# Attention and SwiGLU block on one core: where copies and additions of the query projection are queued

## The chip, the core and the metric

The kernel runs on one core of a Trainium2 chip. A core has five engines that work side by side, each through its own instructions in order: TensorE (PE in the profile; PEld is its weight load), VectorE (DVE), ScalarE (ACT), GpSimd (POOL) and SyncE (SP), which here only issues DMA transfers; ScalarE issues some too. Engines wait for each other by semaphores. The metric is the device time of one execution in microseconds (us), as the median of several runs.

## What is computed

A transformer block of 2048 rows and width 1024, in bfloat16, with six modulation vectors made from a condition `c`:

```python
mod = (_silu(c) @ w_mod).reshape(c.shape[0], 6, 1, -1)
sa, ca, ga, sb, cb, gb = ...
h = _layernorm(x) * (1 + ca) + sa
x = x + ga * _A_ref(h, A_k_cache, A_v_cache, A_wq, A_wo)
h = _layernorm(x) * (1 + cb) + sb
x = x + gb * _B_ref(h, B_w_gate, B_w_up, B_w_down)
```

`_A_ref` is attention with 32 query heads of 128 and 4 key/value heads, over the last 512 positions of the cache; `q = x @ wq`, scores, softmax, times `v`, times `wo`. `_B_ref` is a SwiGLU network, `silu(x @ w_gate) * (x @ w_up) @ w_down`, with an inner width of 3584.

## The kernel before

The rows are worked in four chunks of 512. Each chunk takes the 32 heads in turn, so the attention loop has 128 iterations `i` (`ch, h = divmod(i, Hq)`, from L1135); after head 31 of a chunk comes the output projection (`oproj_plain` in chunk 0, `oproj` after that). The network follows in two stretches of 1024 rows. This text is about the loop.

**The query projection.** From the eighth head on, the projection is made for two heads at once by a scheme of seven products in place of eight (Strassen's, in a variant with fewer additions). `product(p0, m)` (L677) issues product m for the heads p0 and p0 + 1 as four 128x256 matmuls. It takes quarters of the weights, or sums of quarters: `weight_sums` (L646) makes four sums per group of four heads on VectorE, k = 0 to 3, each a 128x1024 subtraction (the line of the helper, L644). The input's sums are made once a chunk by `input_sums` (L669), at heads 27 and 28 for the next chunk.

In chunk 0 all four weight sums of a group are computed, and three of them are also stored to memory (`store_sums`, L658). Chunks 1 to 3 use the same weights again: they fetch the three kept sums (`load_sums`, L662, 768 KB) and compute only the sum k = 1, which needs the fetched k = 0 sum.

The products meet in two PSUM banks, QBK and XBK. Products 1, 6, 5 and 3 add up one after the other in QBK, and after each the running partial sum is copied out: after 1, 6 and 5 to float32 tiles `sn` (`snap`, L702), after 3 straight to the query tile `q` (in `q_fourth`, L740). Products 2, 7 and 4 go to XBK, and VectorE adds a kept partial sum to each (`q_add`, L708; the row is L710). The tracker keeps whole banks apart: a product that writes a bank waits until the copy or addition that reads it is done.

**An iteration's order.** It is written out by hand, and a pair of iterations works for the pair of heads p0, four heads ahead of the scores. Even: `q_first` (the product 4 and its addition that the pair before left in `late`; then product 1, copy), scores of head i + 1 (four 128x512 matmuls), first exp (L764, half of the scores), `q_second` (product 6, copy; product 2, addition), second exp, then `pv` (sixteen 128x129 matmuls for head i, then VectorE's reciprocal L780 and multiplication L781). Odd: `q_third` (product 5, copy; product 7, addition), scores, first exp, `q_fourth` (product 3, copy to `q`; product 4 is left for later), second exp, `pv`. Since every engine works in order, the place of a call in this text is its place in the engine's queue.

Beside these, `run()` and `step()` advance background tasks by one step after `q_first` or `q_third`: layer norms of the next chunk (L428, L376, L377, L437, L392) and the modulation vectors (L1010, L1014), all VectorE. A finished modulation vector goes through `mod_columns` after an odd iteration's `pv`, by matmuls into QBK and a copy out: L1031 on ScalarE for `ga` and `gb`, L1038 or L1041 on VectorE for the others.

**Which engine copies.** `LEAD` is 4 and `Hq` 32. The copies after products 1 and 5 are on ScalarE throughout. Those after products 6 and 3 are on ScalarE while p0 < 36, that is in chunk 0, and on VectorE after that (L706, L748).

**Where sums and loads are queued.** At the end of an iteration, behind `pv` and its multiplication: in chunk 0 one of a group's four weight sums per iteration (L1210 to L1213), and in chunks 1 to 3, every fourth iteration, `load_sums` (L1206 to L1208). In SP's queue that load stands behind `oturn(i - 1)`, a transposing DMA which waits for the multiplication of the head before.

Of the kernel before, what the change touches and what calls it, by code (L numbers as in the profile page):

```python
# [4 lines left out]
AF = mybir.ActivationFunctionType  # L5
# [113 lines left out]
def bass_adaLN_cond__sliding_block_cached__swiglu_ffn__prompt_kernel(  # L119
# [16 lines left out]
    Hq = A_wq.shape[1] // Dh  # L136
# [10 lines left out]
    HG = Hq // 4  # L147
# [9 lines left out]
    T = _Tracker()  # L157
    V, A, G, TE, SP = nc.vector, nc.scalar, nc.gpsimd, nc.tensor, nc.sync
    PE = _Stream(nc.alloc_semaphore("s_pe"), TE, self_exempt=True)
    ACT = _Stream(nc.alloc_semaphore("s_act"), A)  # L160
    DVE = _Stream(nc.alloc_semaphore("s_dve"), V)
# [68 lines left out]
    for i in range(4):  # L230
        for ap_l, b_l, nm, n in ((st_sb, B_st, "st", 12), (mv_sb, B_mv, "mv", 2), (rs_sb, B_rs, "rs", 2)):
            ap_, b_ = small("%s%d" % (nm, i), n, F32)
# [9 lines left out]
    def bank(b, n=512, off=0):  # L242
        return ps[:, b * 512 + off:b * 512 + off + n]
# [18 lines left out]
    with nc.Block() as block:  # L262

        @block.gpsimd
        def _(g):
# [380 lines left out]
            def weight_sums(g, st, e, which):  # L646
                sl = g % NWQ
                w_, bt = wq_sb[sl], B_tq[sl]
                t_ = [tq_[sl][:, n] for n in TQ_AT]
                b11, b12, b21, b22 = w_[:, 0:4, 0:256], w_[:, 0:4, 256:512], w_[:, 4:8, 0:256], w_[:, 4:8, 256:512]  # L650
                for k in which:
                    x, y, extra = ((b12, b11, []), (b22, t_[0], [bt[0]]), (b22, b12, []), (b21, t_[1], [bt[1]]))[k]
                    tt_(st, e, t_[k], bt[k], x, y, ALU.subtract, B_wq[sl] + extra)
# [8 lines left out]
            def load_sums(g):  # L662

                if g >= NCH * HG:
                    return
                ap, bb = kept_sums(g)
                T.op(Q_tq[g % NWQ], lambda: SP.dma_start(ap, wq_t[g % HG]), reads=[B_wqt[g % HG]], writes=bb)
# [31 lines left out]
                        rhs, hb = h_[:, hk, lo:lo + 256], B_h[slot][hk]  # L699
                    mm(out_, lhsT, rhs, kc == 0 and m in (1, 2), kc == 3, [lb, hb], PB[b], loose=True)  # L700

            def snap(st, k):  # L702
                if st is ACT:
                    T.op(ACT, lambda: A.activation(sn[k], bank(QBK, 256), AF.Copy), writes=PB[QBK] + [B_sn[k]])  # L704
                else:
                    T.op(DVE, lambda: V.tensor_copy(sn[k], bank(QBK, 256)), writes=PB[QBK] + [B_sn[k]])  # L706

            def q_add(i, half, off, k):  # L708
                dst = q_sb[i % NQ][:, half * 256:(half + 1) * 256]
# [6 lines left out]
            def q_first(p0):  # L716
                if late:
                    late.pop()()
                if p0 >= NA:
                    return  # L720
                product(p0, 1)
                snap(ACT, 0)

            def q_second(p0):
                if p0 >= NA:
                    return
                product(p0, 6)
                snap(ACT if p0 < Hq + LEAD else DVE, 1)
                product(p0, 2)
                q_add(p0, 0, 0, 0)  # L730

            def q_third(p0):
                if p0 >= NA:
                    return
                product(p0, 5)
                snap(ACT, 2)
                product(p0, 7)
                q_add(p0 + 1, 1, 256, 2)

            def q_fourth(p0):  # L740
                if p0 >= NA:
                    return
                product(p0, 3)
                dst, b_ = q_sb[(p0 + 1) % NQ][:, 0:256], B_q[(p0 + 1) % NQ]
                if p0 < Hq + LEAD:
                    T.op(ACT, lambda: A.activation(dst, bank(QBK, 256), AF.Copy), writes=PB[QBK] + [b_])
                else:
                    T.op(DVE, lambda: V.tensor_copy(dst, bank(QBK, 256)), writes=PB[QBK] + [b_])  # L748

                def last():  # L750
                    product(p0, 4)
                    q_add(p0, 1, 256, 1)

                late.append(last)
# [373 lines left out]
            mod_rest = mod_task([m for k_ in ("cb", "sb", "gb") for m in mods[k_]])  # L1128
            next(mod_ga)
            tasks.append(mod_ga)  # L1130
            ln1 = {}
            ln2 = {}
            o_list = [(k, p) for k in range(2) for p in range(8)]
            o_done = []
            for i in range(NA):  # L1135
                ch, h = divmod(i, Hq)
                p0 = i - i % 2 + LEAD
                if ch == 0 and h in (13, 17, 22):
                    load_wo((13, 17, 22).index(h))
                if ch and h % 2 and 5 <= h < 5 + 2 * AHEAD[ch]:  # L1140
                    load_unit(ch, h // 2 - 2)
                at_xl = [AT_XL + 2 * j for j in range(3)]
                if h == 0 and ch + 1 < NCH:
                    ln1[ch + 1] = ln_task(range((ch + 1) * TPC, (ch + 2) * TPC), False, at_xl, (AT_N, AT_N + 2),
                                          scale=(g1, B_g1, sa, B_sa))
                    tasks.append(ln1[ch + 1])
                if ch == NCH - 1 and h == 3:
                    ln2[0] = ln_task(range(TPC), True, at_xl, (AT_N, AT_N + 2), scale=(g2, B_g2, sb, B_sb))
                    tasks.append(ln2[0])
                if ch == NCH - 1 and h == 10:  # L1150
                    finish(mod_rest)
                    ln2[1] = ln_task(range(TPC, 2 * TPC), True, [AT_FT + 2 * j for j in range(4)],
                                     [AT_MS + 2 * j for j in range(4)], turn=False)
                    tasks.append(ln2[1])
                if ch == NCH - 1 and h == 29:
                    for g_ in list(tasks):
                        finish(g_)
                    for a_ in kept:
                        ln_turn(*a_)
                if h == 26 and ch + 1 < NCH:  # L1160
                    finish(ln1[ch + 1])

                if i + LEAD < PLAIN:
                    qproj(NOP + i // 2, (XBK, QBK)[i // 2], i % 2)
                    if i + LEAD == PLAIN - 1:
                        load_wq(3)
                elif i % 2 == 0:
                    q_first(p0)
                else:
                    q_third(p0)  # L1170
                if ch == 0:
                    for g_ in [ln1[1]] * (i > 3) + [mod_ga] * (i > 2) * (1 if i < 8 else i % 2 if i < 20 else 1 + i % 2):
                        step(g_)
                elif h not in (Hq - 5, Hq - 4):
                    run()
                if i + 1 < NA:
                    scores(i + 1)
                if p0 >= PLAIN:
                    if i % 2 == 0:
                        q_second(p0)  # L1180
                    else:
                        q_fourth(p0)
                exps(i + 1, 2)
                g = (i + 5) // 4
                if i % 4 == 3 and HG + 2 <= g < NCH * HG:
                    weight_sums(g, DVE, V, (1,))
                if h == Hq - 5 and ch + 1 < NCH:
                    input_sums((ch + 1) % 2, (0, 1))
                if h == Hq - 4 and ch + 1 < NCH:
                    input_sums((ch + 1) % 2, (2, 3))  # L1190
                if p0 >= NA:
                    for _ in range(4):
                        o_done.append(o_list[len(o_done)])
                        o_first(ch, *o_done[-1])
                pv(i, mod_columns if i % 2 else lambda: None)
                if i >= 1:
                    oturn(i - 1)
                if i < 3:
                    input_sums(0, ((0, 1), (2,), (3,))[i])
                if i == 1:  # L1200
                    weight_sums(2, DVE, V, (0, 1))

                g = (i + 1) // 4 + 2
                if i % 4 == 3 and i > 3:
                    load_wq(g)
                g = i // 4 + 2  # L1206
                if i % 4 == 0 and g >= HG + 2:
                    load_sums(g)  # L1208
                g = (i + 6) // 4
                for k in range(4):  # L1210
                    g = (i + 7 - k) // 4
                    if i % 4 == (k + 1) % 4 and (3 if k < 2 else 2) <= g < HG + 2:
                        weight_sums(g, DVE, V, (k,))  # L1213
                if i % 4 == 2 and i >= 6 and (i + 2) // 4 < HG + 2:
                    store_sums((i + 2) // 4)
                if h == Hq - 1:
                    oturn(i)
                    if ch == 0:
                        finish(mod_ga)
                        mod_columns()  # L1220
                        next(mod_rest)
                        tasks.append(mod_rest)
                    if ch == NCH - 1:
                        break
                    if late:
                        late.pop()()
                    if ch == 0:
                        oproj_plain()
                    else:
                        oproj(ch, (), lambda: None)  # L1230
# [372 lines left out]
```

## Time and profile before

| | |
|---|---|
| timed runs | 1173.27, 1175.80, 1175.83 us; median 1175.8 |
| profiled execution | 1172.66 us, of which the span from the first to the last instruction is 1170.9 |
| granted TensorE clock | full in all 40 slices |

Busy us in the four attention loops, and in the second half of the program:

| window, us | PE | DVE | ACT | DMA share |
|---|---|---|---|---|
| 30 to 138 (chunk 0) | 104.36 of 108 | 90.83 | 83.42 | 0.97 |
| 195 to 302 (chunk 1) | 104.96 of 107 | 92.50 | 73.57 | 1.02 |
| 352 to 460 (chunk 2) | 105.74 of 108 | 93.05 | 73.89 | 0.96 |
| 509 to 612 (chunk 3) | 101.11 of 103 | 76.33 | 70.78 | 0.97 |
| 660 to 720 (network) | 59.74 of 60 | 49.52 | 28.31 | 0.60 |

Busy time says how long an engine had an instruction in work. It doesn't say whether what it did was waited for: that is in the rows of waits, and, in the rows of a timeline, in the bracket at a row's end, which gives the idle time before it and what ended that. A timeline row gives start, duration, engine, line, operation, what is written and read, and how many instructions were merged.

### The profile page before, as it was taken

The numbers are of one execution on the slowest core, as the hardware profiler recorded it, in microseconds if no ns is written. First come the engines' busy times: TensorE is split into PE (matmuls) and PEld (weight loads), VectorE is DVE, ScalarE is ACT, GpSimd is POOL, SyncE is SP. The second block draws the span as 40 slices with busy tenths as digits, with TensorE's granted clock in tenths as the row PEclk, the third lists the DMA queues.
The fourth block names the chain that finished last, engine by engine and source line by source line (L and its number), as shares of the span: only waits on it lengthen the run. The fifth ranks groups of instructions, "written<-read, shape, count | busy, mean of one in ns | idle before, by whom it ended". The sixth has DMA issues, their size and how long they took to land.

```text
span 1170.9 us, 20809 instructions
## 1 busy us (share of the span) xinstructions
PE 1148.9 (98%) x7789; PEld 668.6 (57%) x7907; DVE 817.6 (70%) x1810; ACT 501.1 (43%) x752; POOL 20.0 (2%) x41
## 2 busy tenths in 40 slices
PE   8999999999999999999999999999999999999998
PEld 5777645777547776468764444444444444444443
DVE  4888746988728988358867688888367777776214
ACT  3777502676206664047651244444210344444110
POOL 1000000000000000000000000000010000000000
PEclk9999999999999999999999999999999999999999
DMA  8999796999869996959969765755886232321733
GB/s 288 262 241 250 192 353 233 292 254 227 279 213 249 274 244 174 334 140 267 267 129 334 247 188 179 216 172 164 278 257 183 81 91 73 108 72 64 260 127 135
DMA packets 283877, 245.58 MB, mean 210 GB/s; under 512 B 109952, under 2 KB 247168, under 8 KB 283776
## 3 DMA queue, kind: packets, MB, share of 16 engines
q1 hardware_dynamic: 253328, 179.74, 58.4%
q10 hardware_dynamic: 30448, 64.50, 15.4%
q8 instruction: 63, 1.03, 0.4%
q14 instruction: 38, 0.31, 0.1%
HBM read 189.27 MB, written 30.41 MB: 188 GB/s over the span
## 4 chain that ended last, share of the span: by engine, by line
PE 94%; DVE 2%; DMA 1%; issue 1%; ACT 1%; ACTq 0%; POOL 0%; DVEq 0%; SPq 0%
PE ps L267 93%; DMA arena<-wq_sums 1%; DMA arena<-in_A_wq_dram 1%; DVE arena L781 0%; DVE arena L644 0%; ACT arena L764 0%; DVE arena L710 0%; PE ps L271 0%; DMA arena<-arena 0%; ACT arena L1031 0%; DVE arena L780 0%; DVE arena L706 0%; DVE arena L983 0%; DVE arena L492 0%; DVE arena L372 0%
## 5 line engine op out<-in xcount | busy, mean ns | idle before, releaser
L267 PE MATMUL ps<-arena 128*128 128x512 bf16 (+5 forms) x7740 | 1146.5, 308 | 16.1 <-DVE arena L710 3.1
L267 PEld LDWEIGHTS ps<-arena 128*128 128x128 bf16 (+1 forms) x7858 | 665.8, 98 | 494.4 <-issue 11.4
L764 ACT ACTIVATE arena<-ps 128x1024 bf16<-128x1024 f32 x256 | 251.2, 1022 | 37.5 <-PE ps L267 34.6
L644 DVE TENSOR_TENSOR arena<-arena 128x512 f16<-128x512 bf16 (+3 forms) x510 | 223.3, 481 | 25.5 <-DMA wo_sums<-arena 12.8
L704 ACT ACTIVATE arena<-ps 128x256 f32<-128x256 f32 x134 | 51.3, 383 | 166.9 <-PE ps L267 165.7
L1309 DVE TENSOR_TENSOR arena<-ps,arena 128x512 f16<-128x512 f32 x112 | 77.3, 690 | 39.8 <-PE ps L267 37.6
L1302 ACT ACTIVATE arena<-ps 128x512 f32<-128x512 f32 x112 | 66.9, 597 | 73.6 <-PE ps L267 73.6
L781 DVE TENSOR_TENSOR arena<-ps,arena 128x512 bf16<-128x512 f32 x128 | 88.5, 692 | 4.5
L983 DVE TENSOR_TENSOR arena<-ps,arena 128x512 f32<-128x512 f32 x34 | 23.4, 689 | 86.7 <-PE ps L267 86.5
L1331 ACT ACTIVATE ps<-ps 128x512 f32<-128x512 f32 x56 | 32.6, 582 | 119.5 <-PE ps L267 119.2
L710 DVE TENSOR_TENSOR arena<-ps,arena 128x256 bf16<-128x256 f32 x180 | 75.6, 420 | 10.9 <-PE ps L267 7.1
L1321 DVE TENSOR_TENSOR arena<-ps,arena 128x512 bf16<-128x512 f32 x56 | 38.5, 688 | 29.6 <-ACT arena L1316 29.6
L780 DVE RECIPROCAL arena<-ps 128x4 f32<-128x4 f32 x128 | 23.1, 180 | 36.4 <-PE ps L267 35.9
L986 DVE TENSOR_TENSOR arena<-ps,arena 128x512 bf16<-128x512 f32 x22 | 15.2, 689 | 45.7 <-PE ps L267 45.7
L1316 ACT ACTIVATE arena<-ps 128x512 f16<-128x512 f32 x56 | 33.3, 594 | 31.6 <-PE ps L267 31.6
L428 DVE BATCH_NORM_STATS2 arena<-arena 128x6 f32<-128x512 bf16 x56 | 38.4, 687 | 8.4 <-DMA arena<-x_mid 8.1
L1014 DVE SCALAR_TENSOR_TENSOR arena<-arena 128x512 f32<-128x512 bf16 x56 | 41.6, 743 | 0.1
L1316 ACT ACTIVATE arena<-arena 128x512 f16<-128x512 f16 x56 | 34.8, 622 | 4.9 <-DVE arena L1309 4.9
L911 DVE TENSOR_TENSOR arena<-arena 128x1024 f16<-128x1024 bf16 (+1 forms) x48 | 29.7, 686 | 6.2 <-DMA arena<-arena 6.2
L935 ACT ACTIVATE arena<-ps 128x512 f32<-128x512 f32 x12 | 6.8, 596 | 60.1 <-PE ps L267 51.4
L379 POOL TENSOR_TENSOR arena<-arena 128x1 f32<-128x1 f32 x30 | 17.5, 584 | 855.1 <-DVE arena L377 855.1
L1321 DVE TENSOR_TENSOR arena<-arena 128x512 bf16<-128x512 f16 x56 | 23.8, 425 | 5.0
(63 smaller groups left out, 221.9 us busy)
## 6 DMA issues: line engine op xcount, KB each, us to landing
arena<-wo_sums ACTq DMA_DIRECT2D x46, 512.0 KB, 7.6
arena<-in_A_wq_dram SPq DMA_DIRECT2D x42, 512.0 KB, 5.4
arena<-wq_sums SPq DMA_DIRECT2D x22, 768.0 KB, 5.8
arena<-in_B_w_gate_dram SPq DMA_DIRECT2D x28, 512.0 KB, 4.0
arena<-in_B_w_up_dram SPq DMA_DIRECT2D x28, 512.0 KB, 5.3
arena<-wd_sums ACTq DMA_DIRECT2D x16, 896.0 KB, 6.5
arena<-in_A_wo_dram SPq DMA_DIRECT2D x24, 512.0 KB, 6.4
arena<-in_B_w_down_dram ACTq DMA_DIRECT2D x12, 896.0 KB, 7.7
```

The lines of the kernel that those rows point to most:

```text
L267: T.op(PE, lambda: TE.matmul(out_ap, lhsT, rhs, start=start, stop=stop, skip_group_check=loose), reads=reads, writes=bb)
L428: T.op(DVE, lambda: V.bn_stats(st_sb[i][:, 6 * hf:6 * hf + 6], x_[:, 512 * hf:512 * hf + 512]), reads=[bx], writes=[B_st[i]])
L644: T.op(st, lambda: e.tensor_tensor(dst, x, y, op), reads=reads, writes=[dst_b])
L704: T.op(ACT, lambda: A.activation(sn[k], bank(QBK, 256), AF.Copy), writes=PB[QBK] + [B_sn[k]])
L710: T.op(DVE, lambda: V.tensor_tensor(dst, bank(XBK, 256, off), sn[k], ALU.add), reads=[B_sn[k]], writes=PB[XBK] + [B_q[i % NQ]])
L764: T.op(ACT, lambda: A.activation(ex[i % NEX][:, kt:kt + 2, :], bank(SCB[kt], 1024).rearrange("p (a b) -> p a b", a=2), AF.Exp, scale=att_s ...
L781: T.op(DVE, lambda: V.tensor_tensor(o_sb[i % NOS].rearrange("p (a b) -> p a b", a=TPC), num, rl_bc, ALU.mult), reads=[B_rl], writes=both + ...
L1014: T.op(DVE, lambda: V.scalar_tensor_tensor(acc, ms[:, kc, :], sc[:, kc:kc + 1], acc, op0=ALU.mult, op1=ALU.add), reads=[B_ms, B_sc, B_acc] ...
L1302: T.op(ACT, lambda: A.activation(fn[m][i], bank(b), AF.Copy), writes=PB[b] + [B_fn[m][i]])
L1309: T.op(DVE, lambda: V.tensor_tensor(ring[c_], bank(b), fn[m][i], ALU.add), reads=[B_fn[m][i]], writes=PB[b] + [bs[c_]])
L1316: T.op(ACT, lambda: A.activation(sl_[c_], src, AF.Silu), reads=reads, writes=writes + [B_sl[c_]])
L1321: T.op(DVE, lambda: V.tensor_tensor(dst, u_[0], s_[0], ALU.mult), reads=[s_[1]] + [x for x in u_[1:]], writes=[db] + list(bb))
```

## The change

`snap` loses its choice of engine, and so does the copy in `q_fourth`: all four copies of a pair are on ScalarE in every chunk. `load_sums` moves from the end of the iteration to a place right after `q_first`, with the same condition, so in SP's queue it now stands ahead of what `run()` issues and of `oturn(i - 1)`. The weight sums of chunk 0 that were issued at the end of an iteration are put in a list, `held`, and issued in the next iteration, after `q_first` or `q_third`, so behind the additions these make and ahead of the step of the background tasks. What is computed stays the same. A line that set `g` and was overwritten at once is dropped.

```diff
-            def snap(st, k):
-                if st is ACT:
-                    T.op(ACT, lambda: A.activation(sn[k], bank(QBK, 256), AF.Copy), writes=PB[QBK] + [B_sn[k]])
-                else:
-                    T.op(DVE, lambda: V.tensor_copy(sn[k], bank(QBK, 256)), writes=PB[QBK] + [B_sn[k]])
+            def snap(k):
+                T.op(ACT, lambda: A.activation(sn[k], bank(QBK, 256), AF.Copy), writes=PB[QBK] + [B_sn[k]])
...
                 product(p0, 6)
-                snap(ACT if p0 < Hq + LEAD else DVE, 1)
+                snap(1)
                 product(p0, 2)
...
                 dst, b_ = q_sb[(p0 + 1) % NQ][:, 0:256], B_q[(p0 + 1) % NQ]
-                if p0 < Hq + LEAD:
-                    T.op(ACT, lambda: A.activation(dst, bank(QBK, 256), AF.Copy), writes=PB[QBK] + [b_])
-                else:
-                    T.op(DVE, lambda: V.tensor_copy(dst, bank(QBK, 256)), writes=PB[QBK] + [b_])
+                T.op(ACT, lambda: A.activation(dst, bank(QBK, 256), AF.Copy), writes=PB[QBK] + [b_])
...
-            ln1 = {}
+            ln1, held = {}, []
...
                     q_first(p0)
                 else:
                     q_third(p0)
+                while held:
+                    held.pop(0)()
+                g = i // 4 + 2
+                if i % 4 == 0 and g >= HG + 2:
+                    load_sums(g)
...
                 if i % 4 == 3 and i > 3:
                     load_wq(g)
-                g = i // 4 + 2
-                if i % 4 == 0 and g >= HG + 2:
-                    load_sums(g)
-                g = (i + 6) // 4
                 for k in range(4):
                     g = (i + 7 - k) // 4
                     if i % 4 == (k + 1) % 4 and (3 if k < 2 else 2) <= g < HG + 2:
-                        weight_sums(g, DVE, V, (k,))
+                        held.append(lambda g=g, k=k: weight_sums(g, DVE, V, (k,)))
```

More of the change, by code (lines that the diff above doesn't have):

```diff
@@ L721, in q_first @@
                 product(p0, 1)
-                snap(ACT, 0)
+                snap(0)
             def q_second(p0):
@@ L735, in q_third @@
                 product(p0, 5)
-                snap(ACT, 2)
+                snap(2)
                 product(p0, 7)
```

## The prediction

> **What bounds the kernel now.** The first page is read from the engines' sums, then the waits of TensorE, then the groups of the operations that the change touches, by shape.
>
> ```profile
> PE 1148.9 (98%) x7789; PEld 668.6 (57%) x7907; DVE 817.6 (70%) x1810; ACT 501.1 (43%) x752; POOL 20.0 (2%) x41
> ```
> ```profile
> PE ps L267 <- DVE arena L710: 3.1, 6, 0.8
> ...
> PE ps L267 <- DVE arena L706: 1.2, 4, 0.3
> ...
> PE ps L267 <- ACT arena L1031: 1.2, 4, 0.3
> ```
> ```profile
> L710 DVE TENSOR_TENSOR arena<-ps,arena 128x256 bf16<-128x256 f32 x180 | 75.6, 420 | 10.9 <-PE ps L267 7.1
> ...
> L704 ACT ACTIVATE arena<-ps 128x256 f32<-128x256 f32 x134 | 51.3, 383 | 166.9 <-PE ps L267 165.7
> ...
> L706 DVE COPY arena<-ps 128x256 f32<-128x256 f32 x46 | 19.3, 420 | 9.2 <-PE ps L267 9.0
> L748 DVE CAST arena<-ps 128x256 bf16<-128x256 f32 x46 | 19.3, 419 | 7.8 <-PE ps L267 6.5
> ```
>
> TensorE is busy 98% of the span, so the change can only win what TensorE loses waiting inside the attention loop. The waits name who it waits for: VectorE's additions (L710) and copies (L706), and the copy at L1031. The idle figures understate the loss. A 128x256 matmul has 273 ns in its row, but in the list of matmuls by time two that follow at once begin 109 ns apart; so an idle gap costs itself plus 0.164 us, and gaps under that don't show as idle at all. I therefore went through TensorE's starts, one after the other, against their usual distance. Undisturbed, two iterations take 3.08 + 3.52 = 6.60 us in all four chunks; what exceeds it I call a loss. Losses in the loop: 2.69 us in chunk 0 behind VectorE and 1.01 us behind L1031; 6.70 us in chunks 1 to 3. The rest of the program is untouched.
>
> **Copies moved to ScalarE** (46 of L706, 46 of L748, all in chunks 1 to 3). VectorE loses 92 x 0.42 = 38.6 us, ScalarE gains 92 x 0.383 = 35.2 us; neither counts by itself, only the waits do. The timeline at 209 us shows the first kind.
>
> ```profile
> 209.48 0.21 DVE L376 BATCH_NORM_AGGREGATE arena<-arena 128x2 f32<-128x12 f32 x1
> 209.72 0.15 DVE L377 TENSOR_SCALAR arena<-arena 128x1 f32<-128x1 f32 x1
> 209.79 0.41 DVE L706 COPY arena<-ps 128x256 f32<-128x256 f32 x1
> ...
> 210.35 1.03 PE L267 MATMUL ps<-arena 128*128 128x256 f16 x8 [0.31 <-DVE arena L706]
> ```
>
> The copy waits behind layer-norm work, and product 5 waits for the copy's bank. ScalarE sits idle for 1.18 us before its next copy at 210.99, so it would have copied in time. Four such losses: 0.479, 0.479, 0.504, 0.448 = 1.91 us. What is late next is the addition behind that copy (L710 at 210.12); without the copies it starts at 209.79 or before, and product 7 is due at about 210.31, so nothing or some 0.04 us remains.
>
> The second kind: L748 late, so product 1 of the next pair, or the mod columns' matmuls, start late: 0.225, 0.138, 0.227, 0.138, 0.129, 0.154, 0.117, 0.186, 0.411 = 1.73 us. At two further places L1038 or L1041 is late behind L748 and a weight sum: 2 x 0.141 = 0.28. All go.
>
> The third kind stands at the end of chunks 1 and 2, where a weight sum and two input sums come together.
>
> ```profile
> 286.86 0.43 DVE L748 CAST arena<-ps 128x256 bf16<-128x256 f32 x1 [0.81 <-PE ps L267]
> ...
> 287.20 2.01 DVE L644 TENSOR_TENSOR arena<-arena 128x1024 f16<-128x1024 bf16 x3
> ...
> 289.94 0.41 DVE L710 TENSOR_TENSOR arena<-ps,arena 128x256 bf16<-128x256 f32 x1
> ...
> 290.50 1.72 PE L267 MATMUL ps<-arena 128*128 128x256 bf16 x22 [0.60 <-DVE arena L710]
> ```
>
> VectorE idles 0.81 us for product 3 ahead of L748 and only then starts the three sums. Without L748 in its queue the sums start some 1.1 us sooner, at about 286.1, and the L710 that now ends at 290.35 ends near 289.3; product 2 is due at 290.50 - 0.77 = 289.73. Both places clear: 2 x 0.768 = 1.54 us.
>
> Against it stands what queues behind the copies on ScalarE: each precedes the second exp of its iteration, and L1031. Per pair ScalarE now does 4 exps of 1.022 (L764) and 2 copies of 0.383, 4.85 us; then 5.62 of the 6.60 us. Chunk 0 already runs with all four copies there, and its undisturbed pairs also take 6.60, with 0.43 us of idle time before most of the first copies. So the exps cost nothing; the margin is 0.98 us a pair, and past it every pair would pay. L1031 does pay: 0.504 us in chunk 0, where L746 is on ScalarE, against 0.415 and 0.416 in chunks 2 and 3; so 2 x 0.09 = 0.18 lost.
>
> A rule speaks against the move: the Trainium skill, "ScalarE: Activation LUTs", Rules for kernel authors, gives plain arithmetic to VectorE, which it calls up to about three times faster per element (bf16, single source). Taken at its ratio, a copy would cost 3 x 0.42 = 1.26 us on ScalarE, a pair 4.85 + 2.52 = 7.37 us, and 46 pairs would lose 35 us. The rows say 383 ns against 420 for these copies, float32 out of PSUM; the rule's case is another, and I take the rows.
>
> **Kept sums fetched sooner** (22 loads, SP's queue). One of them is late enough to matter.
>
> ```profile
> 274.56 0.69 DVE L644 TENSOR_TENSOR arena<-arena 128x1024 f16<-128x1024 bf16 x1 [0.88 <-DMA arena<-wq_sums]
> ...
> 276.55 13.35 PE L267 MATMUL ps<-arena 128*128 128x256 bf16 x134 [0.25 <-DVE arena L710]
> ```
>
> Its load was issued at 265.99, behind a mod-weight load (263.34) and an output transpose (263.93), and landed at 274.44; the sum was ready at about 273.7. Issued right after the query-weight loads it goes out at 263.34 at the earliest, as TensorE's product 4 that frees the buffer is done by about 261. That is 2.65 us for 0.8 needed: 0.42 us saved. The two passed transfers go out 0.53 us later; what the transpose writes is read only at the chunk's end, and its source is one of five tiles in a ring. SP now waits for product 4 with nothing ready behind it: the transpose's own source is done later still. The other 21 loads land in time for all but 0.3 us of VectorE's waiting. Bounds: 0 if the transfers share out the bandwidth as before, 0.42 if not; 0.42 taken.
>
> **Weight sums behind the next additions** (30 sums, chunk 0). Here a sum stands ahead of the late addition that product 2 waits for:
>
> ```profile
> 111.28 0.68 DVE L644 TENSOR_TENSOR arena<-arena 128x1024 f16<-128x1024 bf16 x1
> ...
> 111.87 0.42 DVE L710 TENSOR_TENSOR arena<-ps,arena 128x256 bf16<-128x256 f32 x1
> ...
> 112.44 12.36 PE L267 MATMUL ps<-arena 128*128 128x256 bf16 x124 [0.62 <-DVE arena L710]
> ...
> 120.05 0.42 DVE L710 TENSOR_TENSOR arena<-ps,arena 128x256 bf16<-128x256 f32 x1 [0.77 <-PE ps L267]
> ```
>
> The sum moves the addition by 0.60 us (start to start). The losses at 69.88 (0.379) and 89.91 (0.231) are isolated, VectorE idles 0.3 to 0.4 us after them, so both go: 0.61. The other three (105.05, 112.44, 119.33: 0.996 + 0.784 + 0.304 = 2.08) lie in one stretch in which VectorE never idles, from 103.96, when a query-weight load lands, to 119.28. There its work is the bound and a new order only shifts it: product 7 waits next. At the stretch's end one sum fewer stands ahead of the addition that product 2 waits for, so 119.33 becomes 118.83: 0.50 against the old clock, and up to 0.61 more if the load lands as much sooner as TensorE runs ahead. So chunk 0 gives 0.5 to 1.1, not 2.69; I take 0.8. The sums themselves have at least an iteration to spare before their first product.
>
> **The sum.** 1.91 + 1.73 + 0.28 + 1.54 + 0.42 - 0.18 = 5.70 in chunks 1 to 3, 0.8 in chunk 0: 6.5 us. The profiled execution took 1172.66 us (span 1170.9, 1.8 around it), so 1166.2 like for like. The timed runs are 1173.27, 1175.80 and 1175.83; the profiled one is at the fast end. From the mean of all four, 1174.4, comes 1168 us.
>
> **Rivals.** The forecast: 63%, 1168 us. All of chunk 0's losses go as well (the load lands well ahead): 5.7 + 2.7 = 8.4 us, 1166; for it, half the stretch's stalls follow that one load; against it, VectorE's unbroken run; 15%. Most of the gain is eaten by the next wait: only the L706 kind and one of the others go, some 2.5 us, 1172; for it, VectorE is busy 53.91 of the 60 us from 360 to 420 and additions follow hard on every copy; against it, VectorE is left some 0.8 us emptier per pair; 17%. Slower: ScalarE becomes the pace. Its copy of q also waits for VectorE's addition to the same q tile, and the exp waits behind it; once such waits pass 0.98 us a pair, a copy is exposed each time, 46 x 0.38 = 17.6 us on top of 1168, 1186; it decides from 0.14 us a pair, where the gain is gone. Against it stands chunk 0; 5%.
>
> **The numbers.** This kernel's measurement tells about 0.3%, 3.5 us, from no change. Faster: forecast, first rival and a little of the second, 80%; within: 15%; slower: 5%. The range 1163.5 to 1172.5 holds the first three cases with a run-to-run spread of about 1.5 us to each side.
>
> **What would show it.** Right: no wait of TensorE on L706 or L748 (both rows gone: 180 partial-sum copies and 60 copies of q on ScalarE), the gaps at 290 and 448 us gone, undisturbed pairs still at 6.60 us, L1031's waits some 0.1 us longer in chunks 2 and 3, and chunk 0 shorter by under 1.2 us. Wrong: pairs of chunks 1 to 3 longer than 6.60, TensorE waiting for L764 or L704, or a weight sum waiting for the kept sums still.

## The result

The changed kernel takes 1167.88 us (median of 4 runs, 1166.91 to 1168.69) against 1174.53 before (4 runs, 1172.51 to 1175.83): ratio 0.9945, 95% interval 0.9925 to 0.9964. The profiled executions took 1167.79 and 1172.66 us, with spans of 1165.9 and 1170.9. The forecast was 1168, faster. The changed kernel was profiled a second time, on an execution of 1176.0 us, 8 above that kernel's median and most of it at the program's start and end; of this profile only the chunks are read.

### The profile page after: what moved, and what is told of

Same layout as the page of the kernel before. It is cut to its first block, busy times and chain, and to the rows that moved or that the text cites. A ratio compares the mean times of both kernels' runs of the same rounds, so it can differ in the third digit from the quotient of the medians.

```text
span 1165.9 us, 20810 instructions
## 1 busy us (share of the span) xinstructions
PE 1146.7 (98%) x7789; PEld 669.7 (57%) x7907; DVE 786.7 (67%) x1718; ACT 526.2 (45%) x844; POOL 21.7 (2%) x41
## 3 DMA queue, kind: packets, MB, share of 16 engines
q8 instruction: 63, 1.03, 0.4%
## 4 chain that ended last, share of the span: by engine, by line
PE 95%; DMA 2%; DVE 1%; ACT 1%; issue 1%; POOL 0%; DVEq 0%; ACTq 0%
PE ps L267 95%; DMA arena<-in_A_wo_dram 1%; ACT arena L758 1%; DMA arena<-arena 0%; PE ps L271 0%; DVE arena L775 0%; ACT arena L1025 0%; DMA arena<-in_c_dram 0%; ACT arena L742 0%; DVE arena L977 0%; DVE arena L492 0%; DVE arena L372 0%; DVE arena L707 0%; DVE arena L774 0%; DVE arena L980 0%
## 5 line engine op out<-in xcount | busy, mean ns | idle before, releaser
L758 ACT ACTIVATE arena<-ps 128x1024 bf16<-128x1024 f32 x256 | 262.0, 1027 | 37.6 <-PE ps L267 34.8
L703 ACT ACTIVATE arena<-ps 128x256 f32<-128x256 f32 x180 | 68.7, 382 | 136.7 <-PE ps L267 136.2
L707 DVE TENSOR_TENSOR arena<-ps,arena 128x256 bf16<-128x256 f32 x180 | 75.8, 421 | 32.6 <-PE ps L267 30.4
```

The costliest lines, as they stand in the source:

```text
L707: T.op(DVE, lambda: V.tensor_tensor(dst, bank(XBK, 256, off), sn[k], ALU.add), reads=[B_sn[k]], writes=PB[XBK] + [B_q[i % NQ]])
L758: T.op(ACT, lambda: A.activation(ex[i % NEX][:, kt:kt + 2, :], bank(SCB[kt], 1024).rearrange("p (a b) -> p a b", a=2), AF.Exp, scale=att_s ...
```

## The profile after

Line numbers have moved: the partial-sum copies are L703, the copy to `q` L742, the additions L707, the exps L758, the modulation copy L1025. First the engines' sums, then TensorE's waits, then the groups of the operations that moved, by shape.

```profile
PE 1146.7 (98%) x7789; PEld 669.7 (57%) x7907; DVE 786.7 (67%) x1718; ACT 526.2 (45%) x844; POOL 21.7 (2%) x41
```
```profile
PE ps L267 <- ACT arena L1025: 1.2, 4, 0.3
PE ps L267 <- DMA arena<-arena: 1.1, 2, 0.9
PE ps L267 <- DVE arena L707: 0.8, 2, 0.6
```
```profile
L707 DVE TENSOR_TENSOR arena<-ps,arena 128x256 bf16<-128x256 f32 x180 | 75.8, 421 | 32.6 <-PE ps L267 30.4
...
L703 ACT ACTIVATE arena<-ps 128x256 f32<-128x256 f32 x180 | 68.7, 382 | 136.7 <-PE ps L267 136.2
...
L742 ACT ACTIVATE arena<-ps 128x256 bf16<-128x256 f32 x60 | 22.7, 378 | 0.0
```

VectorE has 92 instructions fewer and ScalarE 92 more. Neither the partial-sum copies nor the copy to `q` hold TensorE any more, and its waits for the additions fell from 3.1 us to 0.8. Look at the end of L707's row: VectorE used to sit idle 7.1 us for TensorE before these additions and is now idle 30.4; it is early where it was late. Two waits of TensorE are for output transposes (`DMA arena<-arena`), after the loop. VectorE's waits for the kept sums, which the sooner loads were to remove, have grown. Before, and below it after:

```profile
DVE arena L644 <- DMA arena<-wq_sums: 1.2, 2, 0.9
```
```profile
DVE arena L644 <- DMA arena<-wq_sums: 2.3, 2, 1.4
```

The same pieces of time can be compared in all profiles by the first matmul of each `pv`: from head 0 to head 31 of each chunk, and from the last `pv` to the end. The projections between the chunks (58.77 and twice 51.86 us) are the same to 0.01 in every run.

| kernel, us | chunk 0 | chunk 1 | chunk 2 | chunk 3 | after the last pv |
|---|---|---|---|---|---|
| before | 104.49 | 104.86 | 105.50 | 101.42 | 559.58 |
| before, second profile | 104.42 | 104.58 | 105.49 | 101.42 | 560.11 |
| changed | 102.51 | 103.59 | 103.52 | 100.19 | 560.91 |
| changed, second profile | 102.46 | 104.76 | 103.52 | 100.19 | 564.79 |
| copies only | 104.62 | 103.87 | 103.51 | 100.19 | 560.87 |
| held sums only | 102.47 | 104.44 | 105.50 | 101.94 | 560.15 |
| sooner loads only | 103.93 | 106.53 | 105.52 | 101.43 | 561.81 |
| changed, loads put back | 102.85 | 103.65 | 103.52 | 100.19 | 561.27 |

In the first pair of profiles the chunks give 1.98 + 1.27 + 1.98 + 1.23 = 6.46 us; the part after the last `pv` takes 1.33 back and the start 0.16, which leaves the spans' 5.0. In the second pair the chunks give 1.96 - 0.18 + 1.97 + 1.23 = 4.98.

## The experiments

### Each part by itself

Copies alone:

```diff
-                snap(ACT if p0 < Hq + LEAD else DVE, 1)
+                snap(ACT, 1)
...
-                if p0 < Hq + LEAD:
...
+                T.op(ACT, lambda: A.activation(dst, bank(QBK, 256), AF.Copy), writes=PB[QBK] + [b_])
```

> Only the two copies are moved to ScalarE. Theory (each part works where the prediction put it): the losses of TensorE in chunks 1 to 3 behind the copies and the three sums go, 1.91 + 1.73 + 0.28 + 1.54 - 0.18 = 5.3 us by matmul starts, chunk 0 keeps its 2.69 us, and the time falls by some 4.5 to 5.5 us (ratio about 0.9955). TensorE, ahead of the old clock, should meet the kept sums' loads sooner, so VectorE's wait for wq_sums should be over the 1.2 us of before. Rival (the gain comes from VectorE having less to do in all, whoever waits): the losses behind the late additions in chunks 1 to 3 shrink in part only, 2 to 3 us. Rival (ScalarE is the pace): pairs of chunks 1 to 3 over 6.60 us.

Measured: 1170.32 us, ratio 0.9970 (0.9958 to 0.9982). Chunks 2 and 3 give all that the changed kernel gives there, 1.99 and 1.23 us, so this gain belongs to the copies alone; no undisturbed pair is over 6.60. Chunk 1 gives only 0.99: VectorE's waits for the kept sums (wq_sums) grew from 1.2 to 3.4 us, as expected, and 1.05 us are lost at iteration 56. The 4.2 us in the three chunks fall short of 5.3.

Held sums alone:

```diff
-            ln1 = {}
+            ln1, held = {}, []
...
                     q_third(p0)
+                while held:
+                    held.pop(0)()
...
-                        weight_sums(g, DVE, V, (k,))
+                        held.append(lambda g=g, k=k: weight_sums(g, DVE, V, (k,)))
```

> Only chunk 0's weight sums are queued behind the next additions. Theory of the prediction: chunk 0 gains 0.5 to 1.1 us, since the stretch with VectorE never idle only shifts. Rival, from the trace after the change: the stretch starts when a query-weight load lands, and that load comes more than 0.61 us sooner, so chunk 0 gains about 2 us and keeps about 0.7. Chunks 1 to 3 keep their 6.7 us of losses in both, unless shifted by the loads. Time 1 to 2 us less, ratio about 0.999.

Measured: 1172.22 us, ratio 0.9991 (0.9983 to 0.9999). Chunk 0 gives 2.02 us, as in the changed kernel; the rival holds. Chunk 3, where nothing was changed, is 0.52 us longer: there a kept sums' load lands late (VectorE waits 0.4 us for it).

Sooner loads alone, and the changed kernel without them. The same lines are moved in both, in the first from the end of the iteration to the place behind `q_first`, in the second from there back to the end:

```diff
+                g = i // 4 + 2
+                if i % 4 == 0 and g >= HG + 2:
+                    load_sums(g)
```

> Only the kept sums' loads are issued sooner. Theory of the prediction: VectorE's waits for wq_sums (1.2 us before) go, the loss before the matmul at 276.55 goes, 0.42 us, and nothing else moves: no difference that the time can tell, ratio 0.9995. Rival (the sooner load shares the DMA engines with what it passed and lands hardly sooner): the waits for wq_sums stay, 0 us. Chunk 0 is unchanged in both.

> The changed kernel with the kept sums' loads put back to the end of the iteration. Theory: with the copies moved, TensorE reaches the sums' deadline sooner, so the later loads are missed more often: VectorE waits for wq_sums 3 us or more in all (2.3 in the changed kernel), and TensorE loses 1 to 3 us more than in the changed kernel. Rival (the load's place is worth nothing): same waits within 0.5 us and the same time as the changed kernel, ratio 0.9945 to before.

Measured: loads alone 1174.85 us, ratio 1.0009 (0.9994 to 1.0024), so no gain and in the profile a loss, 1.7 us in chunk 1 against the first profile of before and 1.9 against the second. The changed kernel without them 1168.75, ratio 0.9956 (0.9944 to 0.9969), which the time can't tell from the changed kernel's; its chunk 1 is 103.65 against 103.59. VectorE waits 2.7 us for wq_sums there and 2.3 in the changed kernel (3.6 in its second profile). The rival holds in both: no gain from the load's place can be seen. The timeline of loads alone shows where its loss is, with a row that the prediction never looked at:

```profile
257.38 0.74 DVE L392 TENSOR_SCALAR arena<-arena 128x512 bf16<-128x512 bf16 x2 [1.93 <-DMA arena<-arena]
258.03 0.42 DVE L706 COPY arena<-ps 128x256 f32<-128x256 f32 x1
...
258.51 4.78 PE L267 MATMUL ps<-arena 128*128 128x256 f16 x43 [1.15 <-DVE arena L706]
```

VectorE waits 1.93 us for a transpose of layer-normed rows, the copy waits behind that, and TensorE behind the copy. The changed kernel waits at the same place, for 1.03 us, but there nothing that TensorE needs is behind it; it loses 5 us later, on the kept sums:

```profile
253.88 0.73 DVE L392 TENSOR_SCALAR arena<-arena 128x512 bf16<-128x512 bf16 x2 [1.03 <-DMA arena<-arena]
...
258.78 0.69 DVE L644 TENSOR_TENSOR arena<-arena 128x1024 f16<-128x1024 bf16 x1 [1.38 <-DMA arena<-wq_sums]
...
260.77 1.45 PE L267 MATMUL ps<-arena 128*128 128x256 bf16 x19 [0.63 <-DVE arena L707]
```

In this pair of kernels two of the 22 loads come near their deadline, those of iterations 48 and 52. Times here are from the first matmul of that iteration's `pv`. The second load is issued at 1.5 us in place of 3.4 (loads put back) and lands at 9.0 in place of 11.9, and its loss goes. The first lands at 11.6 in place of 10.7, and makes a new one. This repeats: in the three profiles with the loads moved the load of iteration 48 lands at 11.5 to 12.5, in the five others of the table at 9.8 to 10.8.

The queue of SP explains a part of it. In the three with the loads moved, the issue of a layer-norm transpose ahead of that load ends at -2.7 us each time, in the other five between -6.9 and -5.0; and the load, "sooner" in the program's order, is issued at 4.5 to 4.6 us. But two of the others issue it later still, at 5.4 and 5.6, and there it lands at 10.6 and 10.8. So the time of issue doesn't settle the landing, and what else does is open.

### What ScalarE can still take

Extra copies to a tile that nothing reads, two and then four behind each moved copy (`more_copies(p0, 2)` or `(p0, 4)` after `snap(1)` and after the copy to `q`):

```diff
+            pad = M.take(205 * KB, [256], F32, [])
...
+            def more_copies(p0, n):
+                for _ in range(n if p0 >= Hq + LEAD else 0):
+                    T.op(ACT, lambda: A.activation(pad, sn[1], AF.Copy), reads=[B_sn[1]], writes=[B_rt[0]])
```

> The changed kernel with four more 128x256 float32 copies a pair on ScalarE in chunks 1 to 3, to a tile that nothing reads, two behind each of the two moved copies. By the prediction's sum of durations (5.62 + 4 x 0.38 = 7.15 us of 6.60) every pair grows by 0.55 us or more, 25 us in all. Rival (ScalarE's instructions overlap, so what counts is start to start: an exp 0.92, a copy 0.27, together 4.8 us, then 5.9): pairs stay at 6.60 and the time stays within 1 us.

> As before with eight more copies a pair, four behind each moved copy. By the sum of durations 8.7 us a pair, 2.1 us longer. By start to start about 7.0, 0.4 us longer, so some 15 to 25 us in all. Either way the pairs of chunks 1 to 3 must now be over 6.60, which shows what a paced ScalarE looks like: TensorE waiting for ScalarE's exp or copies.

Measured, one run each: with four a pair 1174.08 us, with eight 1243.24. ScalarE's rows with four, one odd iteration:

```profile
263.93 1.02 ACT L766 ACTIVATE arena<-ps 128x1024 bf16<-128x1024 f32 x1 [0.18 <-PE ps L267]
264.85 0.38 ACT L749 ACTIVATE arena<-ps 128x256 bf16<-128x256 f32 x1
265.12 0.87 ACT L709 ACTIVATE arena<-arena 128x256 f32<-128x256 f32 x2
265.89 1.01 ACT L766 ACTIVATE arena<-ps 128x1024 bf16<-128x1024 f32 x1
```

An undisturbed pair takes 6.75 us with four and 8.30 with eight, in place of 6.60. How much room ScalarE has in the changed kernel can be read from the idle time before its instructions there:

```profile
282.80 0.38 ACT L703 ACTIVATE arena<-ps 128x256 f32<-128x256 f32 x1 [0.43 <-PE ps L267]
...
283.67 1.02 ACT L758 ACTIVATE arena<-ps 128x1024 bf16<-128x1024 f32 x1 [0.49 <-PE ps L267]
...
286.32 0.38 ACT L703 ACTIVATE arena<-ps 128x256 f32<-128x256 f32 x1 [0.43 <-PE ps L267]
```

With 0.05 more before another exp that is 1.40 us of idle time a pair, so 5.20 of 6.60 are taken. Four extra copies fill a little more than that: from start to start, one takes 0.45 us ahead of another (each waits for the one before it) and 0.32 ahead of an exp, so the four take 1.54. Neither expectation had it. The sum of durations (5.62) is too high, because an exp with an instruction right behind it takes 0.92 us from start to start and a copy 0.26; the sum of those (4.8) is too low, because half of the exps and copies of a pair are followed by a wait, and these count in full.

With eight copies more, what the prediction's slower rival describes comes about. TensorE's row of waits then looks so:

```profile
PE ps L267 <- ACT arena L766: 58.8, 89, 1.3
```

### Chunk 0's remainder

The changed kernel, leaving out the scaling of the next chunk's rows in chunk 0:

```diff
-                                          scale=(g1, B_g1, sa, B_sa))
+                                          scale=(g1, B_g1, sa, B_sa) if ch else None)
```

> The changed kernel without the scaling and shifting of the next chunk's layer-normed rows during chunk 0 (eight instructions pairs at L392 are left out, so chunk 1's queries are computed from unscaled rows). Theory (what chunk 0 still loses near iterations 24 and 25, 0.69 us, is VectorE having too much to do in that stretch, whatever the order): the two losses go, chunk 0 at 101.8 us. Rival (they come from the query-weight load's landing): they stay within 0.2 us.

Measured: both losses are gone, chunk 0 takes 101.74 us (1169.14 us in one run, with a start 1.9 us later; chunk 1 then works on unscaled rows). From 100 to 120 us, this kernel and below it the changed one; a row gives the stretch's length, the busy time of PE, PEld, DVE, ACT and POOL with the number of instructions, the granted clock, the DMA share and GB/s:

```profile
100.00:120.00 20.00, 19.84 (x209) 16.21 (x209) 17.25 (x35) 15.81 (x25) 0.00 (x0) 1.00 0.99 248
```
```profile
100.00:120.00 20.00, 19.49 (x201) 15.51 (x202) 18.93 (x42) 15.48 (x24) 0.00 (x0) 1.00 0.80 227
```

In the changed kernel VectorE is busy 18.93 of 20 us, with no idle time from 99.5 to 117.9; here it is busy 17.25 (17.46 in a stretch shifted by the later start) and idles within the same work. The query-weight load landed 70.2 us after the first `pv`, as in the second profile of the changed kernel, where both losses stand; so the landing isn't their cause.

### The same again

> The changed kernel once more, for a second profile and a tighter ratio. If the gains of chunks 2 and 3 belong to the change they come back to a hundredth (103.52 and 100.19 us from the first to the last pv, against 105.50 and 101.42 before). What hangs on DMA landings should scatter: chunk 0 102.3 to 103, chunk 1 103 to 104, and the part after the last pv 560 to 562 us. Ratio to before 0.995.

> The kernel before, profiled again, to see what of its losses repeats. Chunks 2 and 3 should be 105.50 and 101.42 us to a few hundredths; chunk 0 and chunk 1 within 1 us of 104.49 and 104.86; the part after the last pv between 559 and 562 us, which would say that the 1.3 us by which the changed kernel was longer there is scatter.

Measured: the changed kernel 1167.76 us (median of 6), ratio 0.9949 (0.9935 to 0.9964); before, one run, 1174.05. Chunks 2 and 3 repeat to 0.01 us in both kernels, chunk 0 to 0.07. Chunk 0 doesn't always repeat so closely: with loads alone, where its program is that of before, it takes 103.93, and with the loads put back, where it is that of the changed kernel, 102.85. Chunk 1 of the changed kernel does not repeat: a second missed load, that of iteration 44, adds 1.21 us. The part after the last `pv` scatters: over the other seven profiles of the table it lies between 559.6 and 561.8, and both ends of that come from kernels without the moved copies.

### Versions meant to be better

In the first, the kept sums' load is split and four transposes are spread (`Q_tq2` is a second set of queues for the split load):

```diff
...
-                T.op(Q_tq[g % NWQ], lambda: SP.dma_start(ap, wq_t[g % HG]), reads=[B_wqt[g % HG]], writes=bb)
+                T.op(Q_tq[g % NWQ], lambda: SP.dma_start(ap[:, 0:1024], wq_t[g % HG][:, 0:1024]),
+                     reads=[B_wqt[g % HG]], writes=bb[0:1])
+                T.op(Q_tq2[g % NWQ], lambda: SP.dma_start(ap[:, 1024:3072], wq_t[g % HG][:, 1024:3072]),
+                     reads=[B_wqt[g % HG]], writes=bb[1:3])
...
-                    for a_ in kept:
+                    for a_ in kept[0:2]:
                         ln_turn(*a_)
...
                     oturn(i - 1)
+                if ch == NCH - 1 and h == 30:
+                    ln_turn(*kept[2])
...
                     oturn(i)
+                    if ch == NCH - 1:
+                        ln_turn(*kept[3])
```

> The changed kernel with two edits on DMA alone: the kept sums' load is split, the k = 0 sum (256 KB) first, and the four transposes of layer-normed rows that stand ahead of the last heads' output transposes are spread between and behind them. Theory (what the changed kernel still loses in chunk 1 and after the loop is waiting for these landings): no wait for wq_sums, chunk 1 at 102.7 us or less, and the waits for output transposes at the start of the last projection (1.4 us) down to 0.4, so some 2 us less than the changed kernel, ratio to before 0.993. Rival (the DMA engines are the bound there): the waits move to other landings and the time stays.

Measured: 1167.29 us, ratio 0.9940 (0.9929 to 0.9952), beside 0.9949 for the changed kernel, measured together with it: not told apart. In the profile no wait for wq_sums is left and chunk 1 takes 102.82 us. TensorE's 1.4 us on output transposes went, and 1.46 came back at once. On VectorE eight scalings (2.7 us) stand ahead of the four sums that TensorE needs next, as they do in the changed kernel; TensorE was now there sooner and waited for them.

The second puts eight empty steps ahead of those scalings (and eight later for all that follows on the list):

```diff
-            todo = [lambda kc=kc: ln_scale(1, kc, g2, B_g2, sb, B_sb) for kc in range(DT)] + stretch_todo()
+            todo = [lambda: None] * 8 + [lambda kc=kc: ln_scale(1, kc, g2, B_g2, sb, B_sb) for kc in range(DT)] + stretch_todo()
...
```

> The version with the split load and the spread transposes, and in the last projection everything on the list of background steps comes eight steps later, so that the scalings that wait for the last transpose stand behind the projection's own sums on VectorE. Theory (there they had been put in front of the sums and cost 1.46 us before the f16 product): that wait goes, the part after the last pv is 559 us or less, and the time falls by some 1.3 us against the version before, ratio to before 0.993. Rival (the steps' delay is paid again at the list's end, where the network starts): the same 1 to 2 us come back there.

Measured: 1167.31 us, ratio 0.9940 (0.9921 to 0.9959), no better. The 1.46 us are gone, and TensorE waits for the projection's weights in their place:

```profile
PE ps L267 <- DMA arena<-in_A_wo_dram: 1.9, 2, 1.4
```

No version here beats the changed kernel by more than the measurement tells.

## Why the prediction was right, and where not

**L706 (1.91 us): right.** The four losses are gone, and nothing took their place. The place shown at 209 us before:

```profile
207.58 0.15 DVE L377 TENSOR_SCALAR arena<-arena 128x1 f32<-128x1 f32 x1
207.66 0.42 DVE L707 TENSOR_TENSOR arena<-ps,arena 128x256 bf16<-128x256 f32 x1
```

The addition follows the layer norm at once, and TensorE runs through.

**The three sums (1.54): right.** They start with no copy to wait for, right behind the addition of 283.31:

```profile
283.65 2.01 DVE L644 TENSOR_TENSOR arena<-arena 128x1024 f16<-128x1024 bf16 x3
...
286.40 0.42 DVE L707 TENSOR_TENSOR arena<-ps,arena 128x256 bf16<-128x256 f32 x1
```

**L748 (1.73): right in kind, 0.2 us too much.** All nine losses are gone, but the largest, 0.411, held a matmul whose record is missing from the trace: 0.216 of it was work. Iteration 86 shortened by 0.20.

**L1038 and L1041 (0.28): wrong.** Nothing was won here: iterations 44 and 76 are 0.34 us over an undisturbed one, as before. The copy now waits for TensorE, not for VectorE, and the product behind it starts no sooner:

```profile
231.41 0.16 DVE L1032 TENSOR_SCALAR arena<-ps 128x4 bf16<-128x4 f32 x1 [0.27 <-PE ps L267]
```

**L1031 (0.18 lost): wrong, to the good.** TensorE's loss there is 0.415 us as before, twice. The second exp ends just as L1025's matmuls do:

```profile
419.59 1.03 ACT L758 ACTIVATE arena<-ps 128x1024 bf16<-128x1024 f32 x1
...
420.61 0.60 ACT L1025 ACTIVATE arena<-ps 128x512 bf16<-128x512 f32 x1
...
421.27 0.50 PE L267 MATMUL ps<-arena 128*128 128x256 bf16 x3 [0.25 <-ACT arena L1025]
```

Why chunk 0 loses 0.504 at its own two was not tried; the copy's engine isn't the cause. In chunks 2 and 3 together the working gives 3.3 us, and 3.21 were measured.

**ScalarE as the pace: rightly held unlikely.** The row decided over the rule in the Trainium skill's "ScalarE: Activation LUTs", Rules for kernel authors, whose ratio is for bfloat16: these float32 copies out of PSUM cost 382 ns on ScalarE, not three times VectorE's 420. The margin that the prediction gave, 0.98 us a pair, is 1.40.

**The kept sums' loads (0.42): wrong.** One of the prediction's own signs of being wrong came true, a weight sum that still waits for the kept sums. The prediction followed one load, that of iteration 52, and it did come sooner (it landed at 9.0 us in place of 11.9). The step that failed is that the other 21 loads land in time; this was taken over from the trace before. With the loads moved, the one of iteration 48 lands later, at 11.5 us or more in place of 10.8 or less. Together they are worth 0.06 us in the first profile of the changed kernel, and its second profile loses 1.2 more. The prediction's lower bound, 0, was the value to take.

**Chunk 0 (0.8): right in kind, both terms too small.** The prediction had 0.50 us for the order and up to 0.61 for a query-weight load that lands sooner; 1.98 were measured, past its own limit of 1.2 and three quarters of the way to the rival that had all of chunk 0's losses go. The profiles separate the two terms. By the landing of that load, from the first `pv`:

| chunk 0's program | load lands, us | chunk 0 takes, us |
|---|---|---|
| before | 71.36, 71.29, 71.16, 70.81 | 104.49, 104.42, 104.62, 103.93 |
| sums held | 71.08 | 103.33 |
| sums held | 70.61 | 102.85 |
| sums held | 69.59 to 70.20 (six profiles) | 102.46 to 102.55 |

With the sums held, chunk 0 gets shorter by as much as the load lands sooner, until about 70.2, and no further below that. Carried to the landing of before, 71.36, the two rows above give about 103.6, so the order alone is worth some 0.9 us (an estimate from these rows) and the sooner landing up to 1.1. Why it lands sooner was not settled: in the first pair of profiles it was issued 0.13 us sooner and its transfer was shorter by 1.44, in the second pair it was issued 1.56 sooner and its transfer was longer by 0.46. What is left, 0.7 us, is VectorE's work, as the run without the scaling shows; another order of the same work was not tried.

**After the loop (0): unforeseen.** 1.3 us were lost there in the first pair of profiles, on transposes and projection weights that landed late. The second profile of before has 0.85 us of such a wait too, so most of it is scatter; whether a TensorE that is 6 us ahead meets more of these is open.

In sum, 6.5 was forecast: the chunks gave 6.46 in the first pair of profiles and 4.98 in the second, the medians 6.65 in the first comparison and 5.9 in the second (1173.68 to 1167.76). That the total fits so well is in part luck: in the first pair chunk 0 gave 1.2 us more than the prediction's terms for it, chunk 1 1.1 less.

## What to carry to other kernels

An engine that isn't the bound can still make the bound one wait. Look then for the short instruction that stands behind long, deferrable ones in its queue. Moving it to an engine with gaps, or the deferrable work behind it, wins just the waits, and these can be counted beforehand, by the bound engine's starts against its undisturbed rhythm. Gains that rest on instruction order (chunks 2 and 3) came to 3.21 us of 3.3 and repeated to 0.01 us; gains that rest on when a transfer lands did not repeat. A DMA moved forward in a full issuing queue moves others back, so follow the whole queue over several rounds before giving it a value.

## What the runs showed of the hardware that was not expected

- ScalarE's instructions overlap when one follows another at once: an exp of 1.02 us by its row takes 0.92 from start to start, a copy of 0.38 out of PSUM 0.26. Copies that wait for each other don't: the extra ones, 0.42 by their rows, stand 0.45 apart.
- SP is held by issuing a transpose: in chunk 1 of the changed kernel 1.2 us at least and 3.9 for the layer-norm transpose ahead of iteration 48, against 0.5 for most plain loads. So the time at which the next load goes out can't be read from the program's order alone.
- From the end of its issue, a 768 KB load took 4.1 to 7.9 us to land within one execution of the kernel before, and the query-weight load of the table above 6.2 us there and 4.7 in the changed kernel.
